# Two 512-token units of a tuned H3 + MLP kernel joined into one unit of 1024 tokens

## The chip, the cores and the metric

The kernel runs on one core of a Trainium2 chip. The time is that of one execution on the device, in microseconds (us). Engines are named as the profile names them: PE (TensorE, matmuls), DVE (VectorE), ACT (ScalarE), POOL (GpSimd) and SP (SyncE, which issues all of this kernel's DMA transfers from one queue, in program order).

## What is computed

Two layers with the same weights, each an H3 block (a short and a long causal convolution over the sequence, gated) and an MLP with a squared ReLU, over S = 2048 tokens of D = 1024 channels; the MLP's hidden width is F = 3584. Everything is fp32.

```python
def _A_ref(q, k, v, shift_k, ssm_k, ssm_D):
    k_pad = jnp.pad(k, ((0, 0), (ks - 1, 0), (0, 0)))
    for t in range(ks):
        k_shift = k_shift + k_pad[:, t:t + S, :] * shift_k[:, ks - 1 - t][None, None, :]
    kv = k_shift * v
    y = ...            # causal convolution of kv with ssm_k, per channel, by FFT
    return q * (y + kv * ssm_D[None, None, :])

def _B_ref(x, w1, b1, w2, b2):
    h = jnp.einsum("bsd,df->bsf", x, w1) + b1
    r = jnp.where(h > zero, h, zero)
    h = r * r
    return jnp.einsum("bsf,fd->bsd", h, w2) + b2

x = A_q
x = x + _A_ref(_layernorm(x, axis=-1), A_k, A_v, A_shift_k, A_ssm_k, A_ssm_D)
x = x + _B_ref(_layernorm(x, axis=-1), B_w1, B_b1, B_w2, B_b2)
x = x + _A_ref(_layernorm(x, axis=-1), A_k, A_v, A_shift_k, A_ssm_k, A_ssm_D)
x = x + _B_ref(_layernorm(x, axis=-1), B_w1, B_b1, B_w2, B_b2)
```

## The kernel before, in words

**Units.** Tokens are cut into four blocks of T = 512. A unit is the MLP of one layer for one block; there are eight, worked in the order of `ORDER` (L35): (0,0), (1,0), (0,1), (0,2), (1,1), (0,3), (1,2), (1,3), as (layer, block), and counted from 0 here and in the code. The long convolution's result for a block lies in DRAM (`YD`); the normalised and gated sum with the residual row is formed at the start of a unit's work ("preparation": `prep_a` L735, `combine` L808, then `prep_b` L752 or `prep_w` L814). It ends with the block's rows joined and stored (`X1`), transposed on PE (L854) and split into two fp32r parts, `xh` and `xl` (ACT copy, then a subtraction on DVE, L862). By unit 5 all convolution work is done.

**Matmuls.** Each fp32 product is three fp32r matmuls of high and low parts (`mm3`, L335, matmuls at L336 to L338, always 512 columns wide). A **step** is one weight tile of 128x512 and its twelve matmuls (L336 to L338 four times). The list `steps` holds them in the order of PE; the main loop (`for s, ... in enumerate(steps)`) emits one step after another, and around each step the other engines' instructions that are due then.

**Weights.** Each step needs a pair `whl` (high and low part). `w_advance` (L1031) runs ahead of PE: `w_load` (L989) issues the raw tile's DMA up to 8 steps ahead into a ring of eight buffers `wr`, `w_hi` (L1007) casts it on ACT up to 4 ahead (L1013), and `w_lo` (L1016) makes the low part on DVE up to 3 ahead (L1021), into a ring of six pairs, each reused when its step is done. Some pairs are stored in DRAM once split (`WD`, `w_store` L1025) and later loaded ready-made, 4 steps ahead (`whl<-wd_m`, `whl<-wd_t`).

**Deferred work.** `lag.at(k, fn)` puts a piece of work k steps later; it is emitted there, ahead of that step's weight work, on whatever engines it uses. So each engine's program order follows from the steps at which pieces were put, and an instruction that waits holds up all behind it on its engine.

**Units 5, 6 and 7** (`WINO`) do the first matmul plainly (28 tiles of F by two halves of D, 12 matmuls each: 672) and the second by a seven-product scheme on 2x2 blocks (14 pairs of F tiles, 7 products of 6 matmuls: 588). One block axis of this scheme is the two halves of the unit's tokens, one the two tiles of a pair, one the two halves of D. `relu_w` (L1551) forms the rectified tiles and their sums (L1557 to L1581), `evict_w` adds a product's PSUM banks to its sums in SBUF (L1606, L1608), `merge_w` (L1610) adds those sums up. Four sums of weight tiles for each pair are made once by `make_t` (L1507): w2 is loaded (L1526), summed on DVE, and stored in DRAM as `td` (L1546), from unit 4 on and at a rate per step (`T_RATE`); the pieces' places in SBUF come from `places`.

Of the kernel before, what the change touches and what calls it, by code (L numbers as in the profile page):

```python
# [2 lines left out]

# [16 lines left out]
P = 128  # L20
T = 512
# [30 lines left out]
WINO = (5, 6, 7)  # L52
WMAKE = 4
W_PREP, W_EARLY, W_LATE = 90, (87, 80, 45, 38), 30
T_KEPT, T_RATE, T_FIRST, T_AT = 10, 0.6, 10, (0, 3, 1, 2)
# [185 lines left out]
def tile_h3_mlp(ctx: ExitStack, tc: tile.TileContext, q, kT, vT, shk, ssmT, ssmD, w1, b1, w2, b2,  # L241
# [93 lines left out]
    def mm3(o, lh, ll, rh, rl, start, stop):  # L335
        PE.matmul(o, lh, rh, start=start, stop=False)  # L336
        PE.matmul(o, lh, rl, start=False, stop=False)  # L337
        PE.matmul(o, ll, rh, start=False, stop=stop)  # L338
# [531 lines left out]

    NU = len(ORDER)
# [39 lines left out]
    for u in range(NU):  # L911
        na = AHEAD[u - 1] if u and direct[u - 1] else AHEAD_0 if u == 0 else 0
        if u in WINO:
            add_wino(u)
            continue
# [43 lines left out]
    TD = [dram.tile([P, 4, 512], F32, name=f"td{p}") for p in range(FT // 2)]  # L959

    def split_kept(key):
        k, c, a, i = key
        if k == "t":
# [11 lines left out]
    def room():  # L975
        return len(ring) < RAWS or ring[-RAWS].get("freed", now[0]) < now[0] - 1
# [12 lines left out]
    def w_load():  # L989
# [4 lines left out]
        k, c, a, i = wsrc[w]  # L994
        raws[w] = row()
# [11 lines left out]
    def w_hi():  # L1007
        n = ptr["hi"]
        t = his[n] = mw.tile([P, 2, 512], F32R, name="whl", bufs=6)
        if from_pair(n):  # L1010
            SY.dma_start(t.bitcast(F32), WD[wsrc[n]])
        else:
            A.copy(t[:, 0], raws[n]["t"])  # L1013
        ptr["hi"] += 1
# [16 lines left out]
    def w_advance(s, w):  # L1031
        n = len(wsrc)
        now[0] = s

# [12 lines left out]
        while ptr["load"] < n and ptr["load"] <= w + W_LOAD and (from_pair(ptr["load"]) or room()):  # L1047
            w_load()
# [458 lines left out]
    def make_t():  # L1507
# [3 lines left out]
        def places(n):  # L1511
            if n < T_FIRST:
                nm, m = (("cp", 3), ("cx", 2), ("cg", 2))[n % 3]
                t = cv.tile([P, 2, 2, 256], F32, name=nm, bufs=m)
                return [t[:, 0], t[:, 1]]
            return [pool.tile([P, 2, 256], F32, name=nm, bufs=m) for pool, nm, m in (
                [(cv, "sm", 2)] * 2, [(const, "fh", 1), (const, "fl", 1)], [(ml, "yt", 2)] * 2)[n % 3]]
# [15 lines left out]
        for n, (p, dq) in enumerate(parts):  # L1533
# [9 lines left out]
            if n >= T_FIRST:  # L1543
                yield
# [205 lines left out]

    last_step = {}
    for s, (k, u, *_) in enumerate(steps):
        last_step[u] = s
    start_step = {u: (last_step[u - 1] + 1 if u else 0) for u in range(NU)}
# [26 lines left out]
    for s, (k, u, c, a, i, tts, w) in enumerate(steps):  # L1781
# [3 lines left out]
        if u != cur_u:  # L1785
            cur_u = u
            if u:
                xT = nxt
            bst = {}
            if u in WINO:  # L1790
# [4 lines left out]
            else:  # L1795
# [4 lines left out]
                lag.at(16, add_b2, bst, accs)  # L1800
        soon.tick()
# [7 lines left out]
        behind.tick()  # L1809
        wh, wl = wts[w][:, 0], wts[w][:, 1]  # L1810
        if k == "m1":
# [16 lines left out]
            elif i == 1 and tts[-1] == NT - 1:  # L1828
                lag.at(1, relu2, rs[c, a], 0)
                lag.at(2, relu2, rs[c, a], 1)  # L1830
        elif k == "w2":
# [61 lines left out]
        if u + 1 < NU and not direct[u]:  # L1893
            n = s - start_step[u]
            if n == 28:
                pa = prep_a(*ORDER[u + 1])
            elif n > 28 and pa is not None and next(pa, 0) == 0:
                pa = None
# [10 lines left out]
        if tgen:  # L1909
            town += T_RATE if k == "w2" or u not in WINO and left <= 18 else 1  # L1910
# [73 lines left out]
```

## Time and profile before

| what | value |
|---|---|
| times of three runs | 2705.69, 2709.61, 2710.17 us; median 2709.61 us |
| the profiled execution | 2710.68 us, of which the span of the trace 2708.9 us |
| mean granted PE clock over the span | 0.996 |
| matmul records | 12568 |
| DMA moved | 755.05 MB, mean 279 GB/s |

The page's first part has each engine's busy time, its share of the span and its instructions. The chain is the path followed back from the last instruction; its shares say which engine the end waited for. In the table by stretches the columns are the stretch, its length, then for PE, PEld (weight loads into the array), DVE, ACT and POOL the busy time and count, then the granted PE clock (1 is full), the share of DMA engines busy, and GB/s. In group lines `out<-in` gives the tiles by the program's names; what follows the bar is busy time and the mean of one in ns, then idle time ahead of them and what ended it.

### The profile page before, as it was taken

The page shows a single profiled execution, that of the slowest core. Times are in us where ns is not written, and L with a number is a line of the kernel's source. Part 1 is how long each engine was busy: PE and PEld are TensorE (multiplying, and loading weights), DVE is VectorE, ACT ScalarE, POOL GpSimd, SP SyncE. Part 2 cuts the span into 40 slices and gives each one's busy share as a digit, 9 for nine tenths or more (in the row PEclk, how much of TensorE's full clock was granted, in tenths as well). Part 3 has the DMA queues.
Part 4 walks back from the last instruction along what each step waited for, and adds up shares of the span by engine and source line. Part 5 has one row for each costly group of instructions (what it writes and reads, how often), then busy time and mean ns, then how long its engine had stood idle before and what let it go on. Part 6 is the DMA issues. An engine that isn't in the chain of part 4 may idle for free.

```text
span 2708.9 us, 36533 instructions
## 1 busy us (share of the span) xinstructions
PE 2658.2 (98%) x12568; PEld 2227.5 (82%) x12568; DVE 1988.0 (73%) x3066; ACT 1124.1 (41%) x1936; POOL 845.8 (31%) x532
## 2 busy tenths in 40 slices
PE   7999999999999999999999999999999999999999
PEld 6888787888888888888888888888788788878887
DVE  7878888788987877779677765376787666664565
ACT  3454344433444233442234422244455444445443
POOL 2436565355632655236553454000000010001000
PEclk9999999999999999999999999999999999999999
DMA  8789898699999898788978887789888866676556
GB/s 250 262 305 314 290 311 279 234 308 372 333 305 321 300 342 285 266 334 289 354 263 276 298 304 248 237 295 310 294 286 300 278 231 212 231 270 210 179 167 206
DMA packets 377482, 755.05 MB, mean 279 GB/s; under 512 B 43840, under 2 KB 159184, under 8 KB 377296
## 3 DMA queue, kind: packets, MB, share of 16 engines
q1 hardware_dynamic: 377296, 752.72, 81.6%
q8 instruction: 99, 1.62, 0.2%
q14 instruction: 87, 0.71, 0.1%
HBM read 602.63 MB, written 149.95 MB: 278 GB/s over the span
## 4 chain that ended last, share of the span: by engine, by line
PE 82%; DMA 7%; DVE 6%; issue 2%; POOL 1%; ACT 1%; SPq 1%; DVEq 0%; ACTq 0%; POOLq 0%
PE p L336 25%; PE p L337 25%; PE p L338 25%; DMA wr<-w 2%; PE p L1097 2%; DVE whl L1021 1%; DMA whl<-wd_m 1%; PE pt L336 1%; PE pt L337 1%; PE pt L338 1%; DMA wd_m<-whl 1%; DMA whl<-wd_t 1%; DMA yt<-yd 0%; DMA wd_t<-whl 0%; DMA fx<-kT 0%
## 5 line engine op out<-in xcount | busy, mean ns | idle before, releaser
L526 POOL TENSOR_TENSOR cp<-cx,cg 128x384 f32<-128x384 f32 (+5 forms) x288 | 543.2, 1898 | 569.9 <-DVE sm L530 380.4
L336 PE MATMUL p<-xh,whl 128*128 128x512 f32 (+1 forms) x1840 | 707.6, 385 | 4.3 <-DMA whl<-wd_m 4.2
L338 PE MATMUL p<-xh,whl 128*128 128x512 f32 (+1 forms) x1840 | 703.8, 383 | 0.8 <-POOL whl L1021 0.8
L337 PE MATMUL p<-xl,whl 128*128 128x512 f32 (+1 forms) x1840 | 703.8, 383 | 0.1
L1013 ACT CAST whl<-wr 128x512 fp32r<-128x512 f32 x637 | 383.4, 619 | 437.0 <-PE p L338 308.5
L1021 DVE TENSOR_TENSOR whl<-wr,whl 128x512 fp32r<-128x512 f32 x622 | 500.9, 826 | 73.6 <-ACT whl L1013 69.2
L336 PE MATMUL p<-whl,rh 128*128 128x512 f32 x1372 | 541.2, 394 | 7.3 <-ACT whl L1013 3.7
L337 PE MATMUL p<-whl,rh 128*128 128x512 f32 x1372 | 536.6, 391 | 1.8 <-POOL whl L1021 0.8
L338 PE MATMUL p<-whl,rl 128*128 128x512 f32 x1372 | 536.0, 391 | 0.0
L336 PEld LDWEIGHTS p<-xh,whl 128*128 128x128 f32 x1840 | 347.0, 189 | 71.8 <-DMA whl<-wd_m 3.5
L338 PEld LDWEIGHTS p<-xh,whl 128*128 128x128 f32 x1840 | 346.6, 188 | 68.6 <-POOL whl L1021 1.0
L337 PEld LDWEIGHTS p<-xl,whl 128*128 128x128 f32 x1840 | 346.8, 188 | 65.6 <-DVE xl L1410 0.3
L336 PEld LDWEIGHTS p<-whl,rh 128*128 128x128 f32 x1372 | 258.7, 189 | 62.2 <-DMA whl<-wd_m 4.8
L337 PEld LDWEIGHTS p<-whl,rh 128*128 128x128 f32 x1372 | 258.7, 189 | 56.0 <-DVE whl L1021 3.4
L338 PEld LDWEIGHTS p<-whl,rl 128*128 128x128 f32 x1372 | 258.5, 188 | 54.3
L1504 DVE TENSOR_TENSOR rl<-wr,rh 128x512 fp32r<-128x512 f32 x140 | 145.8, 1042 | 178.3 <-ACT rh L1499 178.2
L1601 POOL TENSOR_TENSOR acc<-acc,px 128x512 f32<-128x512 f32 x18 | 23.2, 1325 | 766.6 <-DMA px<-b 766.6
L530 DVE TENSOR_REDUCE sm<-cp 128x128 f32<-128x384 f32 (+5 forms) x288 | 249.5, 874 | 10.9 <-POOL cp L526 10.9
L1496 ACT ACTIVATE wr<-p,b1t 128x512 f32<-128x512 f32 x138 | 95.2, 690 | 366.8 <-PE p L338 365.8
L1565 DVE TENSOR_TENSOR rl<-wr,rh 128x256 fp32r<-128x256 f32 x84 | 48.9, 582 | 211.2 <-ACT rh L1560 211.1
L1624 DVE TENSOR_TENSOR acc<-p,acc 128x512 f32<-128x512 f32 x152 | 99.8, 686 | 83.4 <-PE p L338 83.4
L1557 ACT ACTIVATE wr<-p,b1t 128x512 f32<-128x512 f32 x84 | 57.9, 689 | 191.0 <-PE p L338 190.9
(277 smaller groups left out, 3304.5 us busy)
## 6 DMA issues: line engine op xcount, KB each, us to landing
whl<-wd_m SPq DMA_DIRECT2D x379, 512.0 KB, 5.4
wr<-w SPq DMA_DIRECT2D x493, 256.0 KB, 5.4
wr<-td SPq DMA_DIRECT2D x152, 256.0 KB, 4.0
wd_m<-whl SPq DMA_DIRECT2D x70, 512.0 KB, 6.1
cx<-xd SPq DMA_DIRECT2D x48, 512.0 KB, 6.0
cg<-gd SPq DMA_DIRECT2D x48, 512.0 KB, 6.8
gd<-fg SPq DMA_DIRECT2D x72, 256.0 KB, 6.5
cx<-xd SPq DMA_DIRECT2D x48, 384.0 KB, 5.7
```

What stands on the lines that cost most here:

```text
L336: PE.matmul(o, lh, rh, start=start, stop=False)
L337: PE.matmul(o, lh, rl, start=False, stop=False)
L338: PE.matmul(o, ll, rh, start=False, stop=stop)
L526: G.tensor_mul(pr.rearrange("p c i -> p i c"), xt[:, 0:j + 1], gt[:, j::-1])
L530: V.tensor_reduce(sm[:, ty, jj], st["pr"], axis=AX.X, op=OP.add)
L1013: A.copy(t[:, 0], raws[n]["t"])
L1021: ENG[e[n % len(e)]].tensor_sub(t[:, 1], raws[n]["t"], t[:, 0].bitcast(F32))
L1097: PE.matmul(o, lh, r, start=start, stop=stop)
L1496: A.activation(r, st["o"], AF.Relu, bias=b1t[:, st["f"]:st["f"] + 1])
L1504: V.tensor_sub(st["lo"], st["r"]["t"], st["hi"].bitcast(F32))
L1557: A.activation(r, st["o"], AF.Relu, bias=b1t[:, st["f"]:st["f"] + 1])
L1624: V.tensor_add(accs[tt][:, d], o, accs[tt][:, d])
```

## The change

Units 5 and 6, that is block 3 of layer 0 and block 2 of layer 1, become one unit of 1024 tokens (`JU = 5`); `WINO` keeps unit 7 alone. Their blocks and layers differ, but the weights are the same. Both matmuls now use the seven-product scheme with the two blocks as one of the block axes, so that each product is 512 tokens wide.

*Phase one* (`ja`, 98 steps: 14 pairs of F tiles, 7 products). The matrix is 2x2 in (token block, half of D), the weights 2x2 in (half of D, tile of the pair). Products 1 and 2, without sums, come first for all pairs (28 steps): product 1 is copied out to DRAM (`PD`) as a seed, product 2 is added to it in PSUM, and the result, rectified, goes to DRAM (`RD[0]`). The seed is later loaded and copied into the bank of product 6. Then come products 6, 5, 7, 4, 3 pair by pair, in a sequence that starts the next pair's product 6 ahead of this pair's 4 and 3 and its 5 and 7 behind them. Their weight tiles are sums of w1 made each time on DVE (`load_part` L1057 loads four tiles, `part_sums` L1045 to L1048), their inputs sums made once from the two blocks' transposed rows (`j_flip`, `j_xsums`, in the steps 11 to 22 of the unit). Four banks' results are rectified, their differences formed (L1948 to L1951) and all seven operands of phase two stored in DRAM (`RD`).

*Phase two* (`jb`, 98 steps: 7 products, in the order `JORD`, by 14 pairs). Each step loads an operand tile from `RD` (8 steps ahead), splits it (`r_hi` on ACT, `r_lo` on DVE, half of the last two products' on POOL), and multiplies by a pair of w2 or `td`. Products 0, 4 and 1 open four banks each; the others go on in four open banks, after which `j_evict` (L2037) adds a finished product's banks to the rows in SBUF (`jacc`, residual rows and b2 loaded and added by steps 7 to 14 of the phase).

Around it: the rows of block 2 for layer 1 are joined and stored during unit 4 (`prep_rows`, from its step 22 on); unit 7 is prepared by `j_next`, put one step behind product 1, from the rows in `jacc`; `make_t` uses other places and in the joint unit the rate `J_RATE` of 1.1. `dynamic_dma_scratch_size=1024` is set, and `mm3` can skip a group check. Unit 7's own steps are as before. In the built program PE has 12,154 instructions before and 11,986 after, DVE 3068 and 2970, ACT 1938 and 1938, POOL 537 and 551, SP 2199 and 2296.

The core of the diff:

```diff
-WINO = (5, 6, 7)
+WINO = (7,)
+JU = 5
+JORD = (0, 4, 5, 2, 1, 6, 3)
+JOPEN = (0, 4, 1)
+JSUM = {0: ((0, 0),), 4: ((1, 1),), 5: ((0, 1),), 2: ((0, 1),), 1: ((0, 0),), 6: ((1, 1),), 3: ((1, 0),)}
+J_PREP, J_SUMS, J_RATE = 22, 3, 1.1
+R_LOAD, R_HI, R_LO = 8, 4, 3
...
+    def add_joint(u):
+        for n in range(0, NP, 2):
+            for kh in range(2):
+                for p in (n, n + 1):
+                    wsrc.append(("m1", 2 * p // FC, 2 * p % FC, kh))
+                    add("ja", u, 0, kh + 1, p, w=len(wsrc) - 1)
+        seq = [(6, 0), (5, 0), (7, 0)]
+        for p in range(NP):
+            more = p + 1 < NP
+            seq += [(6, p + 1)] * more + [(4, p), (3, p)] + [(5, p + 1), (7, p + 1)] * more
+        for j, p in seq:
+            wsrc.append(("s", 0, j, p))
+            add("ja", u, 0, j, p, w=len(wsrc) - 1)
+        for j in JORD:
+            for p in range(NP):
+                f = 2 * p + (j > 0)
+                wsrc.append(("m2", f // FC, int(j == 2), f % FC) if j < 3 else ("t", p, (j - 4) % 4, 0))
+                add("jb", u, 0, j, p, w=len(wsrc) - 1)
...
+    def part_sums(g):
+        s2, s1, s3, s4, w22 = (g[j]["t"] for j in (6, 5, 7, 3, 4))
+        V.tensor_sub(s3, s2, s1)
+        V.tensor_add(s1, s1, w22)
+        V.tensor_sub(s2, s1, s2)
+        V.tensor_sub(s4, s4, s2)
+        g["made"] = True
+
+    def load_part(j, p):
+        if p not in parts:
+            g = parts[p] = {6: row(), 5: row(), 7: row()}
+            for i in (4, 3):
+                g[i] = {"t": ml.tile([P, 512], F32, name="jr", bufs=7)}
+            for i, (f, kh) in {6: (0, 0), 5: (1, 0), 4: (1, 1), 3: (0, 1)}.items():
+                SY.dma_start(g[i]["t"], w1[2 * p + f, :, 4 * kh:4 * kh + 4])
+            pend.append((now[0] + J_SUMS, g))
+        return parts[p][j]
...
+    def j_out(p, nm):
+        st = jst[p]
+        if nm == "22":
+            st["22"] = jrow()
+            V.tensor_add(st["22"], st["e"], st["u3"])
+        elif nm == "12":
+            st["21"] = jrow()
+            V.tensor_add(st["21"], st["e"], st["u2"])
+            st["11"] = jrow()
+            SY.dma_start(st["11"], RD[0][p])
...
+        elif nm == "z":
+            a11, a12, a21, a22 = (st[x] for x in ("11", "12", "21", "22"))
+            st["z0"], st["z3"] = jrow(), jrow()
+            V.tensor_add(st["z0"], a21, a22)
+            V.tensor_sub(a21, a11, a21)
+            V.tensor_sub(a11, st["z0"], a11)
+            V.tensor_sub(st["z3"], a12, a11)
+        else:
+            for j, x in ((2, "z3"), (4, "z0"), (5, "11"), (6, "21")):
+                SY.dma_start(RD[j][p], st[x])
+            del jst[p]
...
+    def j_evict(os, j):
+        for k, h in JSUM[j]:
+            for tt in range(NT):
+                a = jacc[k, tt, h]
+                V.tensor_add(a, os[tt], a)
...
+            if a == 1:
+                lag.at(1, j_p1, o, i)
+            elif a == 2:
+                lag.at(1, j_c11, o, i)
+            elif a == 6:
+                lag.at(1, j_keep, i, "u2")
+            elif a == 7:
+                lag.at(1, j_keep, i, "u3")
+                lag.at(2, j_out, i, "22")
+                lag.at(3, j_out, i, "r22")
+            elif a == 4:
+                lag.at(1, j_out, i, "21")
+            elif a == 3:
+                for d, nm in ((1, "12"), (2, "r12"), (4, "z"), (5, "")):
+                    lag.at(d, j_out, i, nm)
+        elif k == "jb":
+            if s == jb_at:
+                lag.at(8, j_acc_load, 0)
+                lag.at(7, j_acc_load, 1)
...
+            if i == NP - 1:
+                lag.at(1, j_evict, os, a)
+                if a == 1:
+                    lag.at(1, lambda: nxt.append(j_next(ORDER[JU + 2][1], lag)))
+                elif a in (6, 3):
+                    lag.at(3, j_store, int(a == 6))
...
-            town += T_RATE if k == "w2" or u not in WINO and left <= 18 else 1
+            town += J_RATE if u == JU else T_RATE
```

Three places in the built order of the changed kernel. The first is DVE in phase one, within the five steps of one pair: L1045 to L1048 are the weight sums of the next pair, L1109 the split of a weight tile, L1948 to L1951 the differences of a finished pair's operands, and L1930 the addition that frees the bank `p_19181` in which the pair's product 5 stands.

```order
L1045 TENSOR_TENSOR wr<-wr 128x512
L1046 TENSOR_TENSOR wr<-wr,jr 128x512
L1047 TENSOR_TENSOR wr<-wr 128x512
L1048 TENSOR_TENSOR jr<-jr,wr 128x512
L1109 TENSOR_TENSOR whl<-wr,whl 128x512
L1948 TENSOR_TENSOR px<-acc 128x512
L1949 TENSOR_TENSOR acc<-acc 128x512
L1950 TENSOR_TENSOR acc<-px,acc 128x512
L1951 TENSOR_TENSOR px<-acc 128x512
L1930 TENSOR_TENSOR acc<-p_19181,fx 128x512
```

None of these rows exists before. The weight sums stand ahead of the differences, and these ahead of the addition that reads PSUM.

The second is SP in the same steps: L1954 stores the four operands of the pair (`px` and `acc` rows), L1057 loads the four raw w1 tiles of the next pair, L1935 loads the rectified tile of product 2 back, and L1612 is a load of `make_t` (L1526 before).

```order
L1954 DMA rd_9_182<-px 128x512
L1954 DMA rd_9_210<-px 128x512
L1954 DMA rd_9_224<-acc 128x512
L1954 DMA rd_9_238<-acc 128x512
L1057 DMA wr<-w 128x512 x2
L1057 DMA jr<-w 128x512 x2
L1935 DMA acc<-rd_10_155 128x512
L1612 DMA fh<-w 128x2x256
```

These too are new; the loads of the next pair's weights stand behind the stores of this pair on the one queue.

The third is DVE near the end of the joint unit, after product 6 and ahead of product 3: L722, L723 and L901, L902 finish the statistics of unit 7's rows, L819 and L820 join those rows, and L2037 adds product 6's four banks (`p_...` and `pt`) to the sums.

```order
L722 TENSOR_SCALAR rt<-rt 128x1
L723 TENSOR_TENSOR rs<-rs,rt 128x1
L901 TENSOR_SCALAR rn<-rs 128x1
L902 SCALAR_TENSOR_TENSOR rn<-mv_21984,rs 128x1
L819 SCALAR_TENSOR_TENSOR px<-acc,mv,px 128x512
L820 SCALAR_TENSOR_TENSOR acc<-px,rs,acc 128x512
L819 SCALAR_TENSOR_TENSOR px<-acc,mv,px 128x512
L820 SCALAR_TENSOR_TENSOR acc<-px,rs,acc 128x512
L2037 TENSOR_TENSOR yh<-p_20043,yh 128x512
L2037 TENSOR_TENSOR yl<-p_20044,yl 128x512
L2037 TENSOR_TENSOR fy<-pt,fy 128x512
L2037 TENSOR_TENSOR fg<-pt,fg 128x512
```

Before, at the end of unit 5, DVE has the additions of a finished product (L1608) between splits of weights (L1021) and of the next unit's transposed rows (L862):

```order
L1021 TENSOR_TENSOR whl<-wr,whl 128x512
L862 TENSOR_TENSOR xl<-p_19880,xh 128x4x128
L862 TENSOR_TENSOR xl<-p_19885,xh 128x4x128
L1608 TENSOR_TENSOR fg<-p_19861,fg 128x512
L1608 TENSOR_TENSOR fg<-p_19862,fg 128x512
L1021 TENSOR_TENSOR whl<-wr,whl 128x512 x3
```

The preparation's statistics and joins, done long before the end of a unit by `prep_w`, now stand among the last products of the joint unit, ahead of the additions.

More of the change, by code (lines that the diff above doesn't have):

```diff
@@ L2 @@
 from contextlib import ExitStack
+from itertools import chain as chain_of
 import numpy as np
@@ L973, in tile_h3_mlp, with room @@
     tgen, made = [], set()
-    def room():
-        return len(ring) < RAWS or ring[-RAWS].get("freed", now[0]) < now[0] - 1
+    def room(w):
+        n = 3 if wsrc[w][0] == "s" and wsrc[w][3] not in parts else 1
+        return all(len(ring) + k < RAWS or ring[k - RAWS].get("freed", now[0]) < now[0] - 1 for k in range(n))
+    parts, pend = {}, []
+    def part_sums(g):
[14 more added lines that the diff above has]
+        return parts[p][j]
     def row():
@@ L1012, in w_hi @@
         else:
+            while wsrc[n][0] == "s" and "made" not in parts[wsrc[n][3]]:
+                part_sums(pend.pop(0)[1])
             A.copy(t[:, 0], raws[n]["t"])
```

335 lines of the change are left out of this document (315 added, 20 removed).

## The prediction

> **What bounds the kernel now.** I read the page's first part, then its chain, then the three last units by themselves.
>
> ```profile
> span 2708.9 us, 36533 instructions
> PE 2658.2 (98%) x12568; PEld 2227.5 (82%) x12568; DVE 1988.0 (73%) x3066; ACT 1124.1 (41%) x1936; POOL 845.8 (31%) x532
> ...
> PE 82%; DMA 7%; DVE 6%; issue 2%; POOL 1%; ACT 1%; SPq 1%; DVEq 0%; ACTq 0%; POOLq 0%
> ```
>
> TensorE is busy 98% of the span and holds 82% of the chain that ended last: time goes only if matmuls go, and comes back only if TensorE is made to wait. The next view has the units 5, 6 and 7 (counted from 0 as in the code), cut at their first matmuls.
>
> ```profile
> 1826.07:2124.41 298.34, 292.82 (x1293) 240.39 (x1292) 223.93 (x432) 145.15 (x241) 10.66 (x8) 0.99 0.87 301
> 2124.41:2417.12 292.71, 290.74 (x1292) 239.32 (x1293) 191.68 (x348) 140.89 (x233) 10.28 (x8) 1.00 0.70 234
> 2417.12:2708.90 291.78, 287.52 (x1260) 235.98 (x1260) 158.26 (x267) 129.30 (x210) 10.21 (x8) 1.00 0.60 198
> ```
>
> The columns are the stretch, its length, busy time and count on PE, PEld, DVE, ACT and POOL, the granted clock, the DMA share and GB/s. Units 5 and 6 take 591.05 us and hold 2 x 1260 matmuls of 512 columns and 2 x 32 transposes. What one costs is read off the starts:
>
> ```profile
> 1783.67 0.39 PE L336 MATMUL p<-xh,whl 128*128 128x512 f32 x1
> ...
> 1785.03 0.39 PE L336 MATMUL p<-whl,rh 128*128 128x512 f32 x1
> ```
> ```profile
> 2099.65 0.39 PE L338 MATMUL p<-whl,fy 128*128 128x512 f32 x1
> 2099.88 1.03 PE L854 MATMUL p<-ident,px 128*128 128x128 f32 x8
> ...
> 2100.99 0.39 PE L337 MATMUL p<-whl,cx 128*128 128x512 f32 x1
> ```
>
> Six starts apart are 1.36 us, so a matmul takes 0.2267 us and a step of twelve 2.72 us. Eight transposes put 1.34 us where two starts (0.45) would be: 0.89 us. So 2520 x 0.2267 + 8 x 0.89 = 578.4 us are pure work, and 12.65 us are lost. Part of the loss is seen:
>
> ```profile
> PE p L336 <- DMA whl<-wd_m: 6.2, 5, 2.8
> ```
> ```profile
> 1900.00:1910.00 10.00, 7.19 (x32) 5.67 (x31) 9.13 (x17) 3.03 (x5) 2.37 (x2) 1.00 0.64 198
> 1910.00:1920.00 10.00, 10.00 (x39) 8.08 (x38) 4.03 (x8) 4.67 (x7) 0.00 (x0) 0.83 1.00 380
> ```
>
> 6.2 us (first number; five waits, the longest 2.8) are waits for stored weight pairs. After the 2.8 us gap the clock is 0.83 for ten us, which hold 39 starts where 46 are usual (the other whole stretches hold 45 or 46, transposes apart): 7 x 0.2267 = 1.6 us more. The remaining 4.85 us lie in waits too short for the view; I keep them.
>
> **The change part by part: matmuls.** The first matmul goes from 2 x 672 to 14 pairs x 7 products x 12 = 1176, the second stays at 2 x 588 = 1176; the built order has 168 fewer PE instructions and as many transposes. 168 x 0.2267 = **38.1 us off**, on the engine that sets the end. That the change does not do what it says is thereby excluded. Unit 7 keeps its program, and unit 4 gets 58 DVE instructions (joining a block's rows early) in stretches where DVE is under two thirds busy: nothing for both, 1 us if that cover fails.
>
> Everything else is a question of cover. The prices:
>
> ```profile
> L1021 DVE TENSOR_TENSOR whl<-wr,whl 128x512 fp32r<-128x512 f32 x221 | 144.5, 686 | 16.9 <-ACT whl L1013 15.7
> L1013 ACT CAST whl<-wr 128x512 fp32r<-128x512 f32 x220 | 130.9, 619 | 117.1 <-PE p L338 62.8 <-DMA wr<-w 22.4 <-DMA wr<-td 10.7
> ...
> L812 DVE SCALAR_TENSOR_TENSOR px<-px,rs 128x512 f32<-128x512 f32 x16 | 12.0, 752 | 0.6
> L811 DVE SCALAR_TENSOR_TENSOR px<-px,mv 128x512 f32<-128x512 f32 x16 | 11.9, 746 | 1.2 <-DMA px<-yd 1.2
> ```
> ```profile
> 1873.24 2.49 DVE L1021 TENSOR_TENSOR whl<-wr,whl 128x512 fp32r<-128x512 f32 x4
> ```
> ```profile
> wr<-w SPq DMA_DIRECT2D x58, 256.0 KB, 6.0
> ```
> ```profile
> whl<-wd_m SPq DMA_DIRECT2D x40, 512.0 KB, 6.7
> ```
> ```profile
> DMA to landing us min/median/max: 4.2/5.5/8.6
> ```
> ```profile
> 1977.07 0.55 SPq L1526 DMA_DIRECT2D fh<-w  x1
> ...
> 1980.35 0.49 SPq L1546 DMA_DIRECT2D td<-yt  x1
> ```
> ```profile
> 600.00:650.00 50.00, 49.89 (x232) 41.32 (x231) 49.76 (x63) 22.08 (x39) 34.57 (x20) 1.00 1.02 372
> ```
>
> A 512-wide DVE operation lasts 0.686 us and, back to back, takes 0.60 (four in 2.49 with 0.686 for the last); an ACT cast 0.62. A weight tile of 256 KB lands 6.0 us after its issue in unit 5 and a stored pair 6.7; the stores of `td` take 4.2 to 8.6. SP issues one DMA in 0.55 us when its queue is full (six from 1977.07 to 1980.35). The most that the queues carried over 50 us is 372 GB/s.
>
> **Phase one, first 28 steps** (the two products of the unsummed blocks). By the order and the tile sizes the first 14 steps issue 17.8 MB (stores of unit 4, rows of block 2, stored weight pairs, `PD`, `RD[0]`). At 372 GB/s that is 47.8 us against 41.7 us of TensorE: 6.1 us behind. A stored pair is asked for four steps (10.9 us) ahead and lands in 6.7, which covers 4.2: **2 us** of wait, between 0 (the queue is emptier) and 6. Beside it the sums of the inputs are made in four quarters, 11 DVE and 6 ACT operations each. In the twelve steps that hold them DVE has 49 wide operations and 12 of half width: 49 x 0.60 + 12 x 0.4 = 34 us, in 12 x 2.72 + 3 x 0.89 = 35.3 us. It just fits; ACT's copies of the first product, for which TensorE waits one step later, stand behind casts that wait for DVE. **1 us**, between 0 and 4 (38.7 us of DVE if nothing overlaps).
>
> **Phase one, five products per pair.** Five steps, 13.6 us, per pair. DVE has 15 wide and about 4.4 half operations, 10.8 us: enough. But there is a round: the last difference of a pair's operands (L1951) releases SP's four stores (L1954), the four raw weight tiles (L1057) stand behind them on SP, DVE's weight sums (L1045 to L1048) wait for these, and the next pair's operands (L1948 to L1951) stand behind the sums on DVE, with L1930 behind, for which TensorE's product 3 waits. Its length: 7 issues x 0.55 = 3.9, landing 6.0, the last sum 0.7, one weight split 0.6, four operations 2.6, and 0.1 to wake: 13.9 us, 0.3 more than the period. Over 13 pairs 4 us, and 0.8 more in each of four pairs where two pairs of `make_t` operations stand in the round, less the 1.8 us that it starts ahead: **5.4 us**. With the landing at 4.2 it is nothing, with 8.6 it is 13 x 2.9 + 1.4 = 39 us. I take 6.0: same size, same source, same unit, a DMA share of 0.87.
>
> **The seam between the phases.** In steps 692 to 698 (the first seven of phase two) SP issues 10.5 MB: the last pairs' stores, seven stored pairs, operands, `td`. At 372 GB/s 28.2 us, in 19.0 us of matmuls: 9.2 behind, 4.2 of it covered as above: 5.0 us, and one dip of the clock, 1.6: **6.6 us**. The 4.2 MB of residual rows behind them are not wanted before step 706, and tiles asked for eight steps ahead have 21.8 us. Bounds 0 and 12.7 + 1.6 (18.9 MB over 14 steps, 50.8 against 38.1). [...]
>
> **From product 6 to product 3.** Both accumulate in the same four banks, so product 3 waits until DVE has added product 6 to its sums (L2037). On DVE these four stand behind the preparation of unit 7:
>
> ```profile
> 1889.07 1.28 DVE L697 BATCH_NORM_STATS2 st<-px 128x6 f32<-128x512 f32 x2
> 1890.38 0.21 DVE L698 BATCH_NORM_AGGREGATE mv<-st 128x2 f32<-128x12 f32 x1
> ```
> ```profile
> L713 DVE SCALAR_TENSOR_TENSOR rt<-rs,ve 128x1 f32<-128x1 f32 x8 | 1.8, 220 | 0.3
> ...
> L711 DVE RECIPROCAL rs<-sd 128x1 f32<-128x1 f32 (+1 forms) x10 | 1.6, 159 | 0.0
> ```
>
> A block of statistics is 1.28 + 0.21 + 0.16, a join four operations of 0.75, a scale and bias six small ones, 1.1. From step 770 to the sums of 776 that is, with the weight and operand splits: 3.6 + 2.85 + 4.7 + 2.85 + 4.7 + 2.85 + 4.1 = 25.65 us, in six steps of 16.3. DVE can be some 1.7 steps (4.6) ahead, since its splits wait for weight buffers that TensorE frees, and the first sum needs 0.7: **5.4 us** of wait and 1.6 for the clock. Bounds 0 (DVE much further ahead) and 10 + 1.6.
>
> **The sum**, against the profiled execution's own 2710.68 us: 2352 x 0.2267 + 7.1 + 4.85 + (2 + 1 + 5.4 + 6.6 + 5.4 + 1.6 = 22.0) = 567.1 us in place of 591.05: 23.9 less. The median shown is 2709.61, so **2686 us**.
>
> **Rivals.** *All hidden*: the queues run shallower than I count and only some 4 us of the 22 are left: 42 less, 2668. For it: TensorE stood at 49.89 and 50.00 of 50 us at 372 and 352 GB/s in units that asked for as much. Against: the joint unit asks for it in bursts.
> *The round sets the pace, mildly*: landing near 7.5 us, 1.8 per pair instead of 0.3, 20 us more: 2705. For it: rows of 6.7 and 8.6.
> *The round sets the pace, and the kernel is slower*: at 8.6 us each pair waits 2.9 us, as long as the gap at 1900 to 1910 behind which the clock fell, 1.6 more each: 39 + 13 x 1.6 = 60 us in place of 5.4, so 2740. Without dips it decides against the change from a loss of 29.3 us on, 2.15 us per pair, a landing of 7.85 us for the last weight tile. For it: four stores and four loads, 2.1 MB, go out together, 5.6 us at 372 GB/s. Against: the median of 6.0 at the same load.
> [...]
>
> **How the numbers follow.** Forecast (2676 to 2698) 0.55, all hidden 0.17, mild pace 0.16, slower 0.12. The range takes in the hidden case and the mild one: 2667 to 2711, with some 0.15 left out above and 0.04 below. About 0.2% (5.4 us) is what a measurement of this kernel can tell from no change. Faster by more: 0.55 + 0.17 + half of the mild case = 0.80; within: 0.09; slower: 0.11.
>
> **What would show it.** 168 fewer matmuls than before; unit 7 at some 292 us; the joint unit near 567. Right or wrong by step: waits of p<-whl for `wd_m` in the first 14 steps and at the seam; per pair five steps of 13.6 us, or more with L1045 waiting for `wr<-w` and product 3 for L1930; a wait of product 3's first matmul for L2037; clock below 1 behind each. The forecast is wrong if a wait stands in every pair, or if the waits at the three seams are missing.

## The result and the profile after

The changed kernel takes 2698.4 us in the median of six runs (2697.3 to 2704.5), the one before 2710.3 (six runs, 2705.7 to 2712.6): a ratio of 0.9962, with a 95% interval of 0.9949 to 0.9975. That is 10 to 12 us less, where 23.6 were forecast. The direction was right and the time lies in the range of 2667 to 2711, but the gain is half of what was forecast.

The profiled execution takes 2697.74 us. Its page begins, and its chain ends, like this:

```profile
span 2695.9 us, 36188 instructions
PE 2625.7 (97%) x12400; PEld 2199.5 (82%) x12400; DVE 1972.1 (73%) x2968; ACT 1112.2 (41%) x1936; POOL 869.8 (32%) x546
...
PE 74%; DVE 10%; DMA 9%; issue 2%; SPq 2%; ACT 1%; POOL 1%; DVEq 0%; ACTq 0%; POOLq 0%
```

The 168 matmuls are gone (12568 to 12400), and PE's busy time with them, 32.5 us. But PE holds 74% of the chain where it held 82%, and DVE 10% where it held 6%: TensorE now waits. The next view has the joint unit and unit 7, cut at their first matmuls, in the columns that were shown of before (stretch, length, PE, PEld, DVE, ACT, POOL, clock, DMA share, GB/s):

```profile
1826.82:2403.62 576.80, 551.31 (x2417) 452.31 (x2416) 370.76 (x621) 271.52 (x469) 42.49 (x30) 0.98 0.82 286
2403.62:2695.90 292.28, 287.42 (x1261) 235.76 (x1259) 159.59 (x269) 129.65 (x210) 10.21 (x8) 1.00 0.58 193
```

The joint unit takes 576.8 us in place of 591.05, 14.25 less; the units ahead of it end 0.75 later and unit 7 is 0.5 longer. All of the result is in the joint unit, and so is the miss, since 567.1 was forecast. Its bare work is 540.3 us (2352 matmuls of 0.2267 and 7.1 for transposes), so 36.5 are lost. The waits that the view of waits names add up to 25.2 of them (engine, line, what it waited for, total, times, longest):

```profile
PE p L345 <- DVE whl L1109: 7.9, 1, 7.9
PE p L344 <- DVE yh L2037: 7.4, 1, 7.4
PE p L344 <- ACT fx L1924: 4.7, 2, 4.0
PE p L344 <- DMA whl<-wd_m: 3.0, 1, 3.0
PE p L344 <- DVE acc L1930: 1.3, 2, 0.9
PE p L346 <- DVE cx L1989: 0.9, 1, 0.9
```

Four single gaps make nearly all of it. Each has a slow clock behind it, 7 to 11 starts 0.43 us apart, which the starts of PE show, here behind the gap of 3.0 us:

```profile
1851.75 0.80 PE L344 MATMUL p<-xh,whl 128*128 128x512 f32 x1 [3.00 <-DMA whl<-wd_m]
...
1853.20 0.63 PE L344 MATMUL p<-xh,whl 128*128 128x512 f32 x1
1853.62 0.63 PE L345 MATMUL p<-xl,whl 128*128 128x512 f32 x1
```

Seven starts stand 0.40 to 0.60 us apart instead of 0.2267; that is 1.5 us more. In what follows a loss is the time by which starts stand further apart than 0.2267, so gap and slow clock together:

| place in the joint unit | forecast us | measured us |
|---|---|---|
| first 14 steps, a stored weight pair (at 1848) | 2 | 4.8 |
| sums of the inputs | 1 | 0 |
| first pair of the five products, copies on ACT (1905, 1917) | none of its own | 0.4 + 6.6 |
| rounds of the later pairs (L1930, L1924) | 5.4 | 3.1 |
| seam, the first seven steps of phase two (2113 to 2132) | 6.6 | 0 |
| start of product 4 (2159 to 2179) | none of its own | 11.7 |
| from product 6 to product 3 (2353) | 7.0 | 9.2 |
| the small rest | 4.85 | 0.7 |
| sum | 26.85 | 36.5 |

**Where each gap comes from**, read from the chain followed back from it (start, length, piece). At 1848 a stored pair stands on SP behind four loads of block 2's rows, 2 MB, and lands 9.50 us after its issue instead of the 6.7 that the forecast used; the issue itself came 6.5 us before TensorE began to wait (the gap of 3.00 ends at 1851.75), not 10.9:

```profile
1839.20 0.63 SPq L1848
...
1840.83 0.57 SPq L1848
...
1842.21 9.50 DMA whl<-wd_m
...
1851.75 0.80 PE p L344
```

At 1917 it is the raw weights of pair 1, issued at 1910.66: an ACT cast (L1101) waits for their sums; the copy that TensorE wants (L1924) stands behind this cast:

```profile
1910.66 0.43 SPq L1057
...
1911.14 5.05 DMA wr<-w
...
1916.31 0.70 DVE wr L1045
...
1917.76 0.70 DVE wr L1047
...
1918.49 0.62 ACT whl L1101
...
1920.84 0.52 ACT fx L1924
...
1921.41 0.79 PE p L344
```

The round of the later pairs is there as forecast: stores, loads, landing, split, differences. The load that closes the round shown here is one of `make_t` (L1612), issued behind the four weight loads:

```profile
1970.37 0.70 DVE px L1951
...
1971.09 0.33 SPq L1954
...
1974.72 0.43 SPq L1057
...
1975.20 0.55 SPq L1612
...
1975.79 4.91 DMA fk<-w
...
1984.33 0.70 DVE px L1951
```

From one L1951 to the next are 13.96 us, against 13.6 of matmuls; 13.9 was forecast. After the first one the rounds up to 2083 last 13.7 to 14.9 us. The longest of these, from 1998.58 on, is closed by a weight tile, which lands after 4.2 us and for which DVE waits (L1046).

The seam that the forecast named costs nothing: in the first seven steps of phase two TensorE never waits, while the queues carry 403 GB/s (the last number), more than the 372 that the forecast took for the most they carry:

```profile
2112.63:2131.67 19.04, 19.04 (x85) 15.77 (x84) 10.67 (x18) 6.70 (x12) 0.00 (x0) 1.00 1.05 403
```

The largest gap, at 2159, stands at the start of the second product, 14 steps into the phase, and has another cause. On DVE the four additions of product 0 (L2037) stand apart, each behind POOL, and the split L1109 that TensorE waits for stands behind them:

```profile
2158.05 0.69 DVE L2037 TENSOR_TENSOR acc<-p,acc 128x512 f32<-128x512 f32 x1 [1.77 <-POOL acc L2024]
2160.51 0.69 DVE L2037 TENSOR_TENSOR acc<-p,acc 128x512 f32<-128x512 f32 x1 [1.77 <-POOL acc L2024]
2162.96 0.69 DVE L2037 TENSOR_TENSOR acc<-pt,acc 128x512 f32<-128x512 f32 x1 [1.76 <-POOL acc L2024]
2165.41 0.69 DVE L2037 TENSOR_TENSOR acc<-pt,acc 128x512 f32<-128x512 f32 x1 [1.76 <-POOL acc L2024]
2166.02 1.13 DVE L1109 TENSOR_TENSOR whl<-wr,whl 128x512 fp32r<-128x512 f32 x1
```
```profile
2156.71 9.89 POOL L2024 TENSOR_TENSOR acc<-acc,px 128x512 f32<-128x512 f32 x8 [464.52 <-DMA wr<-td]
```

POOL is adding b2 to the same rows (L2024), two operations for each row tile, one every 1.24 us. It began only at 2156.71, because the load of b2 stands on SP behind the 4 MB of residual rows and lands 5.9 us after its issue, at some 2156.2. (For POOL's idle time the row above names another load, `wr<-td`; b2 itself landed half a microsecond before POOL began.) The first row is SP's issue, the second the load's size and time to landing:

```profile
2150.27 0.43 SPq L1825 DMA_DIRECT2D px<-b  x1
```
```profile
px<-b SPq DMA_DIRECT2D x1, 512.0 KB, 5.9
```

From product 6 to product 3 the place and the queue are as forecast: the last operation ahead of L2037 on DVE is a join of unit 7's rows, which ends when TensorE has waited for nearly seven us:

```profile
2358.91 0.75 DVE L820 SCALAR_TENSOR_TENSOR acc<-px,rs,acc 128x512 f32<-128x512 f32 x1
2359.57 0.69 DVE L2037 TENSOR_TENSOR yh<-p,yh 128x512 f32<-128x512 f32 x1
```

One of the small operations ahead of it is much longer than forecast. L721 (L713 before) took 0.22 us in the prediction's row; here it takes 1.20 to 1.24, three times in the six steps ahead of the gap, and each time it ends together with a POOL operation:

```profile
2354.84 1.27 POOL L1989 TENSOR_TENSOR cx<-rh,cx 128x512 fp32r<-128x512 f32 x1 [7.03 <-DVE cp L1989]
```
```profile
2354.92 1.20 DVE L721 SCALAR_TENSOR_TENSOR rt<-rs,ve 128x1 f32<-128x1 f32 x1
```

That is 3.0 us of DVE that the forecast did not count.

### The profile page after: what moved, and what is told of

It reads as the page before. It is cut to its first block, busy times and chain, and to the rows that moved or that the text cites. A ratio compares the mean times of both kernels' runs of the same rounds, so it can differ in the third digit from the quotient of the medians.

```text
span 2695.9 us, 36188 instructions
## 1 busy us (share of the span) xinstructions
PE 2625.7 (97%) x12400; PEld 2199.5 (82%) x12400; DVE 1972.1 (73%) x2968; ACT 1112.2 (41%) x1936; POOL 869.8 (32%) x546
## 4 chain that ended last, share of the span: by engine, by line
PE 74%; DVE 10%; DMA 9%; issue 2%; SPq 2%; ACT 1%; POOL 1%; DVEq 0%; ACTq 0%; POOLq 0%
PE p L344 22%; PE p L345 22%; PE p L346 22%; DMA wr<-w 3%; PE p L1187 2%; DVE whl L1109 2%; DMA whl<-wd_m 1%; PE pt L344 1%; PE pt L345 1%; PE pt L346 1%; DMA wd_m<-whl 1%; DVE sm L538 1%; DMA cg<-gd 1%; DVE st L705 0%; PE pt L400 0%
## 5 line engine op out<-in xcount | busy, mean ns | idle before, releaser
L344 PE MATMUL p<-xh,whl 128*128 128x512 f32 (+1 forms) x1504 | 576.6, 383 | 3.8 <-DMA whl<-wd_m 3.7
L346 PE MATMUL p<-xh,whl 128*128 128x512 f32 (+1 forms) x1504 | 572.4, 381 | 0.8 <-POOL whl L1109 0.8
L345 PE MATMUL p<-xl,whl 128*128 128x512 f32 (+1 forms) x1504 | 572.4, 381 | 0.1
L1109 DVE TENSOR_TENSOR whl<-wr,whl 128x512 fp32r<-128x512 f32 x524 | 444.6, 861 | 120.0 <-ACT whl L1101 118.4
L1101 ACT CAST whl<-wr 128x512 fp32r<-128x512 f32 x539 | 328.9, 620 | 437.7 <-PE p L346 271.1
L344 PE MATMUL p<-whl,rh 128*128 128x512 f32 x1204 | 475.3, 395 | 5.5 <-ACT whl L1101 4.4
L345 PE MATMUL p<-whl,rh 128*128 128x512 f32 x1204 | 470.7, 391 | 1.7 <-DVE whl L1109 1.1
L346 PE MATMUL p<-whl,rl 128*128 128x512 f32 x1204 | 470.4, 391 | 0.0
L344 PEld LDWEIGHTS p<-xh,whl 128*128 128x128 f32 x1504 | 283.5, 188 | 57.2 <-DMA whl<-wd_m 4.5
L346 PEld LDWEIGHTS p<-xh,whl 128*128 128x128 f32 x1504 | 283.1, 188 | 55.5 <-POOL whl L1109 1.0
L345 PEld LDWEIGHTS p<-xl,whl 128*128 128x128 f32 x1504 | 283.5, 188 | 52.2 <-DVE xl L1500 0.3
L344 PEld LDWEIGHTS p<-whl,rh 128*128 128x128 f32 x1204 | 227.2, 189 | 52.5 <-ACT whl L1101 5.3
L345 PEld LDWEIGHTS p<-whl,rh 128*128 128x128 f32 x1204 | 227.1, 189 | 48.4 <-DVE whl L1109 2.3
L538 DVE TENSOR_REDUCE sm<-cp 128x128 f32<-128x384 f32 (+5 forms) x288 | 249.8, 874 | 11.7 <-POOL cp L534 11.7
L1586 ACT ACTIVATE wr<-p,b1t 128x512 f32<-128x512 f32 x138 | 95.3, 690 | 357.1 <-PE p L346 354.4
L2024 POOL TENSOR_TENSOR acc<-acc,px 128x512 f32<-128x512 f32 x8 | 9.9, 1281 | 464.5 <-DMA wr<-td 464.5
L684 POOL TENSOR_TENSOR sm<-sm 128x512 f32<-128x512 f32 x48 | 69.2, 1441 | 129.6 <-DVE sm L538 116.7
L1587 ACT ACTIVATE wr<-wr 128x512 f32<-128x512 f32 x140 | 88.8, 634 | 4.4
```

The source lines that it names most:

```text
L344: PE.matmul(o, lh, rh, start=start, stop=False, skip_group_check=skip)
L345: PE.matmul(o, lh, rl, start=False, stop=False, skip_group_check=skip)
L346: PE.matmul(o, ll, rh, start=False, stop=stop, skip_group_check=skip)
L538: V.tensor_reduce(sm[:, ty, jj], st["pr"], axis=AX.X, op=OP.add)
L684: E.tensor_add(s[:, 1:3], s[:, 1:3], s[:, 0:1].to_broadcast([P, 2, s.shape[2]]))
L1109: ENG[e[n % len(e)]].tensor_sub(t[:, 1], raws[n]["t"], t[:, 0].bitcast(F32))
```

## The experiments

The theory: each gap is an instruction that waits ahead of one that TensorE needs on the same engine; the gaps have separate causes, and what one costs comes back when it is cured. The rival: the joint unit has too little room altogether (DMA traffic, DVE time), and a cured gap opens again elsewhere. All kernels start from the changed one (2698.4); each time is a median, with its ratio to the kernel before on the same chip. The losses of all of them by place (us, as in the table above; "product 4" is all that is lost from the eighth step of phase two to the end of product 4). Each row is one execution, and a place that an edit does not touch still varies: 1848 from 3.4 to 7.0, the rounds from 3.1 to 5.2.

| kernel | joint unit | 1848 | ACT, 1917 | rounds | product 4 | 6 to 3 |
|---|---|---|---|---|---|---|
| changed | 576.8 | 4.8 | 7.0 | 3.1 | 11.7 | 9.2 |
| 1 additions of product 0 late | 572.8 | 4.3 | 7.4 | 4.7 | 6.0 | 9.4 |
| 2 own buffer for product 2's tile | 571.8 | 3.4 | 0 | 5.6 | 12.3 | 9.8 |
| 3 unit 7's rows spread | 570.3 | 4.4 | 6.1 | 5.2 | 11.4 | 2.3 |
| 4 rows of block 2 late | 579.7 | 3.7 | 8.2 | 5.0 | 12.2 | 9.8 |
| 5 b2 on DVE | 569.3 | 7.0 | 6.1 | 3.5 | 1.4 | 10.2 |
| 6 as 2, stores behind loads | 566.9 | 4.4 | 0 | 1.0 | 11.6 | 9.7 |
| 7 make_t rests | 579.4 | 1.3 | 3.9 | 6.6 | 16.8 | 10.0 |
| 8 combination | 547.4 | 4.6 | 0 | 0.9 | 1.4 | 0 |
| 9 casts late | 579.1 | 6.3 | 3.1 | 8.4 | 10.9 | 9.7 |
| 10 combination, make_t rests | 549.5 | 1.6 | 0 | 1.0 | 6.4 | 0 |

**1. The additions of product 0 ten steps late**

```diff
-                lag.at(1, j_evict, os, a)
+                lag.at(1 if a else 10, j_evict, os, a)
```

> One change: the four additions of product 0's banks (L2037) are put ten steps behind the product instead of one. Theory: the 8.1 us gap at the start of product 4 (2158.87 to 2167.20) is DVE standing at L2037 for POOL's b2 additions to the same rows (L2024), with the weight and operand splits queued behind it. Then the gap goes, and 8.1 + 1.45 + about 1.9 of slow clock behind it with it: 9 to 11 us less than the changed kernel's 2698, so 2687 to 2690; DVE operations beside POOL's additions should still last 1.7 to 1.8 us instead of 0.69. Rival (what the prediction had for the seam): the queues are behind, 10.5 MB in seven steps, and the splits wait for weights and operands anyway: the gap moves to DMA releasers and under 3 us come back.

Measured: 2694.5 us, ratio 0.9946 (0.9931 to 0.9961). The gap of 8.1 us is gone, and in its place stand eight waits of 0.3 to 1.0 us, 3.4 us apart: 6.0 us of loss. DVE has this at that place:

```profile
2157.79 0.68 DVE L1989 TENSOR_TENSOR cp<-rh,cp 128x512 fp32r<-128x512 f32 x1
...
2162.36 1.77 DVE L1109 TENSOR_TENSOR whl<-wr,whl 128x512 fp32r<-128x512 f32 x1
2164.06 1.78 DVE L1989 TENSOR_TENSOR cp<-rh,cp 128x512 fp32r<-128x512 f32 x1
```

The same operation takes 0.68 us ahead of POOL's additions and 1.78 beside them. Two such operations a step are 3.4 us in a step of 2.72, which is the distance of the waits. So DVE's wait for POOL was the gap, as the theory had it, but a second cost lay under it, and the gain is 4 us, not 9 to 11. The rival is wrong too: TensorE waits for DVE at each of them, and for no DMA.

**2. An own buffer for product 2's tile**

```diff
-        x = row()
-        rectify(x["t"], o, 2 * p)
-        SY.dma_start(RD[0][p], x["t"])
-        drop(x)
+        t = mkfx([P, T])
+        rectify(t, o, 2 * p)
+        SY.dma_start(RD[0][p], t)
```

> One change: the rectified tile of product 2 goes into an fx buffer instead of a row of the weight ring. In the built program the raw weights of pair 1 are then loaded 8 steps ahead of their use instead of 5. Theory: the 4.2 us gap at 1917 is ACT standing at the cast of pair 1's summed weight (L1101), which waits for DVE's sums and these for the load issued at 1910.66, with the copy that TensorE waits for (L1924) queued behind it. Then this gap goes, with its 2.3 us of slow clock: 5 to 7 us less, 2691 to 2693. Rival: the queue is so full there that the earlier load lands as late, or the first pair's own loads move the wait: under 2 us.

Measured: 2694.4 us, ratio 0.9944 (0.9929 to 0.9959). The wait for L1924 at the first pair is gone, and its 7.0 us with it; the one that is left is that of the last pair.

```profile
PE p L344 <- DVE acc L1929: 3.1, 3, 1.6
...
PE p L344 <- ACT fx L1923: 0.7, 1, 0.7
```

The earlier load was enough: its late issue was the cause. The rounds lose 2.5 us more than in the changed kernel (5.6 in place of 3.1), so the time is 1.4 above the expectation; that the gap had given them time is likely and not shown.

**3. Unit 7's rows three steps apart**

```diff
-                lag.at(d + 2 * tt, early, tt, k)
+                lag.at(d + 3 * tt, early, tt, k)
...
-                lag.at(d + 2 * tt, late, tt, k)
+                lag.at(d + 3 * tt, late, tt, k)
```

> One change: the joins and statistics of unit 7's four row tiles are put three steps apart instead of two. Theory: the 7.6 us gap between product 6 and product 3 is the queue of these operations on DVE ahead of the additions (L2037). One join with statistics and one more join, about 7 us of DVE, then stand behind the additions: the gap falls to 0 to 2 us and its slow clock (1.5) goes: 6 to 9 us less, 2689 to 2692. Rival: DVE is short of time in the whole stretch and the delay only moves, to the start of unit 7, whose first matmuls then wait for the last rows: no gain, 2697 to 2700.

Measured: 2692.1 us, ratio 0.9929 (0.9911 to 0.9948). The wait for L2037 falls from 7.4 to 2.1 us, as the theory had it, and no slow clock follows it (starts 0.31 us apart, then 0.22 to 0.23):

```profile
PE p L344 <- DVE yh L2037: 2.1, 1, 2.1
```

Unit 7 does not start late for it: from its first matmul to the end are 291.5 us. For this gap the theory holds.

**4. The rows of block 2 three steps late**

```diff
-                lag.at(5, j_rows_load, jb)
+                lag.at(8, j_rows_load, jb)
...
-                    lag.at(8 + tt // 2, j_rows_norm, rn, tt)
-                    lag.at(11 + 3 * tt, j_flip, tt)
+                    lag.at(11 + tt // 2, j_rows_norm, rn, tt)
+                    lag.at(14 + 3 * tt, j_flip, tt)
```

> One change: loading block 2's rows (2 MB), flipping them and summing them is put three steps later in phase one. Theory: the 3.2 us gap at 1848 is a stored weight pair issued at 1842.21 behind the 2 MB of rows, landing after 9.5 us. Then it lands in 6 to 7, the gap falls to 0 to 1 us and its 1.5 us of slow clock goes: 3 to 5 us less, 2693 to 2695. Rival: the traffic of the stretch as a whole is above what the queues carry (17.8 MB in 14 steps), and another pair waits a few steps later: no gain, 2697 to 2699.

Measured: 2699.4 us, ratio 0.9967 (0.9954 to 0.998): no gain. The pair at 1848 is no longer late, but one 8 us further into the unit is, by 2.4 us, and a third by 0.7. Here the rival was right: not the 2 MB ahead of one pair, but the traffic of these steps.

**5. b2 on DVE, a row tile a step**

```diff
-    def j_b2(st, k):
-        for tt in range(NT):
-            for h in range(2):
-                a = jacc[k, tt, h]
-                G.tensor_add(a, a, st["t"][:, h * 512:(h + 1) * 512])
+    def j_b2(st, k, tt):
+        for h in range(2):
+            a = jacc[k, tt, h]
+            V.tensor_add(a, a, st["t"][:, h * 512:(h + 1) * 512])
...
-                lag.at(13, j_b2, bst, 0)
-                lag.at(14, j_b2, bst, 1)
+                for n in range(2 * NT):
+                    lag.at(14 + n, j_b2, bst, n // NT, n % NT)
```

> One change: b2 is added to the residual rows by DVE, one row tile (two operations) a step in the steps 14 to 21 of phase two, instead of by POOL all at once from step 13 on. The additions of product 0 then stand ahead of them and wait for the rows alone. Theory: of the 11.7 us lost at the start of product 4, 8 to 9 were DVE waiting for POOL (gone when only the additions were put later), and the 6 that stayed there when the additions were put later are DVE operations that last 1.7 us beside POOL's instead of 0.69. Then both go: 9 to 12 us less than the changed kernel's 2698, 2686 to 2689, against 2694.5 for the later additions alone. Rival: the 6 us that stayed there are the queues (weights and operands late); then they stay here as well, and it comes to some 2694.

Measured: 2689.3 us, ratio 0.9927 (0.9911 to 0.9944). The start of product 4 loses 1.4 us where it lost 11.7. In the program the first tile's two additions of b2 stand ahead of product 0's (I had expected them behind), which costs little:

```profile
2156.77 1.29 DVE L2023 TENSOR_TENSOR acc<-acc,px 128x512 f32<-128x512 f32 x2 [0.26 <-DMA px<-b]
2157.98 1.28 DVE L2036 TENSOR_TENSOR acc<-p,acc 128x512 f32<-128x512 f32 x2
2159.18 1.28 DVE L2036 TENSOR_TENSOR acc<-pt,acc 128x512 f32<-128x512 f32 x2
2160.37 0.68 DVE L1109 TENSOR_TENSOR whl<-wr,whl 128x512 fp32r<-128x512 f32 x1
```

Sixteen more operations on DVE cost less than sixteen on POOL beside it, and DVE's stay at 0.68. With experiment 1 this shows that both costs at this place were POOL's: DVE waiting for it, and DVE slowed beside it. The rival, late weights and operands, is excluded, for the loads are the same and their wait is not there.

**6. Product 2's own buffer, and a pair's stores behind the next loads**

```diff
-                for d, nm in ((1, "12"), (2, "r12"), (4, "z"), (5, "")):
+                for d, nm in ((1, "12"), (2, "r12"), (4, "z"), (6, "")):
```

> The own buffer for product 2's rectified tile, and the four operand stores of a pair (L1954) one step later, so that they stand behind the next pair's weight loads on SP. Theory: the waits of 0.8 to 1.6 us for L1930 in every second or third pair are the round of stores, loads, sums and differences, 14.3 us against 13.6. Without four issues of 0.5 us it is 12.4, so these waits go: some 4 us less than with the own buffer alone (2694.4), 2690 to 2691. Rival: the row buffers that the stores free are then what the next differences wait for; the waits stay or grow, 2694 to 2700.

Measured: 2687.6 us, ratio 0.9921 (0.9906 to 0.9937). The waits of the rounds, 3.1 us for L1929 in experiment 2, are gone (the 1.0 of the table is the last pair's L1923), and nothing waits for row buffers. That the stores stood ahead of the loads on SP is what made the round too long. The median is 6.8 us below experiment 2, more than was expected; in the profiled executions 4.9 of the difference lie in the joint unit, 4.6 of them in the rounds.

**7. make_t rests in the first 14 steps**

```diff
-            town += J_RATE if u == JU else T_RATE
+            town += J_RATE if u == JU and s >= start_step[u] + 14 else 0 if u == JU else T_RATE
```

> One change: the making of the w2 sums (make_t) rests in the first 14 steps of the joint unit, which takes some 3.5 MB of loads and stores out of the stretch. Theory: the stored weight pair at 1848 is late because of the traffic as a whole (moving 2 MB of rows by three steps did not help). Then with 3.5 of 17.8 MB gone the 4.8 us there fall to 0 to 2: 3 to 5 us less, 2693 to 2695. Rival: the pair is late because SP issues it late, behind stores that wait for ACT and DVE; then it stays, 2697 to 2699.

Measured: 2698.9 us, ratio 0.996 (0.9945 to 0.9975). The loss at 1848 falls from 4.8 to 1.3 us. The pair is issued no earlier (15.5 us into the joint unit, 15.4 in the changed kernel) but lands after 7.41 us in place of 9.50: the traffic made it late, as the theory had it, though the late issue is still there. The work put off is paid in the rounds (6.6 in place of 3.1) and around the start of product 4 (16.8 in place of 11.7). Neither expectation was right for the whole: the place was understood, and the gain was lost elsewhere.

**8. The combination** of 2, 3, 5 and the later stores, with product 6's additions ahead of the step's other work:

```diff
-                lag.at(1, j_evict, os, a)
+                (soon if a == 6 else lag).at(1, j_evict, os, a)
```

> All that has helped or should: own buffer for product 2's tile, b2 on DVE, unit 7's rows three steps apart with product 6's additions ahead of the step's other work, operand stores one step later. Theory (each wait has a cause of its own): of the 36.7 us above the bare matmuls in the joint unit 6.7 + 11 + 9 + 3.5 go, some 6 to 8 stay: 2698 - 29 = 2667 to 2674. Rival (the waits only move): the gains do not add up, 2680 to 2688.

Measured: 2669.4 us (2668.2 to 2670.9), ratio 0.9853 (0.9838 to 0.9868): faster than both kernels.

```profile
1827.26:2374.64 547.38, 542.97 (x2417) 449.00 (x2416) 371.13 (x637) 271.65 (x469) 19.38 (x14) 1.00 0.86 301
```
```profile
PE p L344 <- DMA whl<-wd_m: 2.9, 1, 2.9
PE p L345 <- DVE whl L1109: 0.7, 1, 0.7
PE p L344 <- ACT fx L1923: 0.7, 1, 0.7
```

The joint unit takes 547.4 us for 540.3 of bare work, 43.7 less than units 5 and 6 before. The gains add up, so for these four places the theory holds against the rival: there was room for all of it, at the same DMA share or more (0.86, against 0.82). Product 6's additions put first were run only here, not by themselves.

**9. ACT's casts of summed weights two steps ahead instead of four**

```diff
-            return w + (W_PAIR if k < n and from_pair(k) else W_HI) + (phase[0] == "x")
+            return w + (W_PAIR if k < n and from_pair(k) else 2 if k < n and wsrc[k][0] == "s" else W_HI) + (phase[0] == "x")
```

> One change: ACT's casts of summed weights are put two steps ahead of their use instead of four; the loads of pair 1 stay as late as they are. In the program the copy that TensorE waits for at 1917 (L1924) then stands ahead of the cast that waits for DVE's sums. Theory (queue order on ACT): the wait for L1924 goes, but one step later TensorE waits for the summed weight itself, since its load is as late as before: of the 4.2 us and 2.3 of slow clock 2.7 to 4 come back, 2694 to 2696; and the rounds, with less lead on the weights, wait as often or more. Rival (the load alone sets it): no change, 2697 to 2699.

Measured: 2700.9 us, ratio 0.9967 (0.9955 to 0.998). The 7.0 us on ACT fall to 3.1, now as waits for the weight itself, as the theory said; but the shorter lead costs 5.3 more in the rounds, so the kernel as a whole gains nothing, where 2 to 4 us were expected. With the load as late as before, then, 3.9 of the 7.0 us were the order on ACT and 3.1 remain; the earlier load of experiment 2 takes away all of it.

**10. The combination with make_t's rest**

> The combination (2669.4) and the rest of make_t in the first 14 steps. Theory: the wait for the stored weight pair at 1848, 4.6 of the 7.6 us that are left, is the traffic of these steps, and with the other waits gone there is room for make_t's loads and stores later: 3 to 4.5 us less, 2665 to 2667. Rival: as alone, the traffic only moves: new waits at the seam and in the rounds eat it, 2668 to 2671.

Measured: 2670.5 us, ratio 0.9862 (0.9847 to 0.9877): no better than 2669.4. Some 3.0 us come back at 1848, and 5.0 are lost again around the start of product 4, in part to stored pairs. The rival was right: this one gap only moves.

## Why the prediction was right or wrong

- **The matmuls**: right. 168 fewer, and with the waits cured the joint unit takes 43.7 us less than its two units, the 38.1 of the matmuls and 5.6 of the losses of before.
- **First 14 steps**: right that a stored pair comes late in heavy traffic, 4.8 us in place of 2. The pair landed after 9.5 us, not 6.7, and was issued 6.5 us ahead, not 10.9: 7.2 us behind in place of 6.1, of which the forecast's 4.2 are covered, so 3.0 of wait. The slow clock behind it, 1.55 us, had no term here.
- **Sums of the inputs**: nothing is lost there; 1 us was forecast.
- **The round**: right in its chain, 3.1 us in place of 5.4. That its length came out at 13.96 us for a forecast of 13.9 is in part luck. The loads shown landed after 4.2 and 4.9 us, not 6.0, and more issues and more work on DVE stood in the round than were counted. The 0.55 us of an issue was misread (from 1977.07 to 1980.35 are five issues, 0.66 each), and no row shows that the queue was full there; in the round nine issues took 4.7 us, 0.52 each.
- **The first round**: it had no term. The forecast let it start 1.8 us ahead; in fact pair 1 follows pair 0 after three steps, its loads went out only five steps ahead, and ACT's cast held L1924: 7.0 us. The forecast had named this very chain, a copy behind a cast that waits for DVE, but priced it only in the twelve steps of the input sums.
- **The seam**: the step that failed, "9.2 behind". In these seven steps nothing is lost, at 403 GB/s where 372 were taken as the most (over 630 to 680 the trace of before has 385 itself). In its place stands a loss that the forecast had put at nothing: 11.7 us at the start of product 4, where L2037 waits for POOL's b2 additions on the same rows (8.1 us) and DVE's splits last 1.75 to 1.78 us beside them in place of 0.68; with b2 on DVE 1.4 are left. The forecast priced L2037 only ahead of product 3, and b2's additions on POOL nowhere.
- **Product 6 to product 3**: right in mechanism and place, 9.2 us in place of 7.0; the wait was 7.4 in place of 5.4. The rows show three operations (L721) that last 1.0 us longer than counted, each beside a POOL operation; no run takes POOL's part away there, so this is read and not tested.
- **The small rest**: 4.85 us were carried over from before, and only 0.7 are there. This error hid part of the others.

The forecast was 9.7 us short in the joint unit: 11.7 for product 4, 7.0 for the first round, 2.8 for the start and 2.2 for product 6 to 3, less 6.6 for the seam, 3.3 for the rounds and the sums and 4.15 for the rest. That the time still lies in the range owes something to luck: terms that were too high by 14 us stood against terms that were too low or missing by 24. Apart from the first 14 steps it was not bandwidth that was short but the order of work on SP, ACT, DVE and POOL; the slower rivals, with landings of 7.5 and 8.6 us in the rounds, did not come true.

## What to carry to other kernels

For each instruction that a change adds, ask what it waits for and what stands behind it on its engine, also on engines with much idle time: POOL was busy 7% of the joint unit, and what waited for it or ran beside it at the start of product 4 was a third of the loss. A pipeline's first rounds want their own sum, since their lead is not that of the steady state. Here the gaps with separate causes could be cured one by one, and the gains added up; the one gap made of traffic only moved.

## What the runs showed of the hardware

Beside POOL's additions (L2024) the splits L1109 and L1989, DVE operations with both inputs in SBUF, took 1.75 to 1.79 us each, but for the first in each run (1.13 in the changed kernel, 0.94 in experiment 1); without them they took 0.68, in the changed kernel from 2180.62 on, when POOL had ended at 2180.15, and in experiment 1 ahead of the additions. Beside these splits the two streams stand at one operation of each every 1.70 us. L2037, with one input in PSUM, kept its 0.69 beside the additions, and these stood 1.22 to 1.25 us apart. L721, with two inputs of 128x1, took 1.20 to 1.24 us beside one POOL operation of 1.27 to 1.30, against 0.22 for the same operation before. What the two engines share in these cases no run shows.

In the joint units of the changed kernel and of experiments 2 to 10, gaps between two starts that stood alone and lasted 2.2 us or less cost no clock (2.22 in experiment 3, 2.15 in experiment 7, beyond 0.2267). Gaps of 2.35 to 3.2 mostly cost 7 to 9 matmuls at 0.43 us, some 1.5 to 2 us (2.62 in experiment 6, 3.16 in the changed kernel), though one of 2.82 in experiment 2 and one of 2.53 in experiment 4 cost none. Longer gaps cost little more: 7 to 14 matmuls behind 3.5 to 4.6 us, 7 to 12 behind 7.6.
